# A linear-attention and mixture-of-experts kernel: the diagonal of the scores by two-column products from r*k instead of scaled copies of r

## The chip, the core and the metric

The kernel runs on one core of a Trainium2 chip. A core has five engines with a queue of instructions each: TensorE (PE in the profile; its weight loads are PEld), VectorE (DVE), ScalarE (ACT), GpSimd (POOL) and SyncE (SP), which here issues most of the transfers (DMA). They work at the same time and wait for one another by semaphores. SBUF is the memory on the chip, PSUM the one that TensorE writes. The metric is the device time of one execution in microseconds (us).

## The reference

r, k and v have the shape (4 sequences, 8 heads, 768 tokens, 48). The first half is a recurrence for each sequence and head, with a state of 48x48, a decay w and a bonus u for the token itself:

```python
for t in range(S):
    cur = einsum('bhd,bhe->bhde', u[None] * kt, vt)
    y[:, :, t] = einsum('bhd,bhde->bhe', rt, state + cur)
    state = w[None, :, :, None] * state + einsum('bhd,bhe->bhde', kt, vt)
```

The second half sends the 3072 resulting rows of 384 values through a mixture of experts: a row takes part if its product with w_skip is above 0; it goes to the one of 8 experts with the largest gate value, y = relu(x w1) w2 with 1024 hidden values, and y, weighted by the gate, is added to it.

## The kernel before

**Steps.** The scan cuts the 768 tokens into 12 chunks of 64 and takes two sequences at a time: 2 x 12 = 24 steps, numbered n = 0 to 23. In a step the recurrence becomes products of matrices. The 8 heads are 4 pairs `hp` with two halves `a`; 48 dimensions are padded to 64, so the two halves of a pair fill 128 partitions. `q` is the sequence within the pair of sequences.

**One step.** `prep_r` and `prep_k` multiply the loaded r and k (tile `dm`) by powers of the decay (`w_d`) and make `rd` and `kd`. `scores` multiplies `kd` by `rd` into the PSUM tile `ps_p`, 16 products of 64x64 weights in four quarters of the array. `mask_scores` copies from there into `am` what lies where a token looks at an earlier one (mask `below`) and, for the token itself, from a second half of the columns (mask `eye`). That second half is the product with r times the bonus: `rd` holds two versions of r side by side, and the second is made from the first by VectorE for two head pairs (second part of `prep_r`, L420) and by ScalarE for the other two (`bonus`, L406). `across` adds the products of `rd` with the carried state `sblk` to `ps_y`, `within` those of `am` with v (tile `vz`); `evac` copies `ps_y` out and sends it to memory. `turn_k` transposes `kd` into `ps_l`, and ScalarE copies it to `kt` for the update of the state in `state` (`ps_s`). `turn_x` transposes the finished rows of the step before for the gates. Gates and routing are spread over the steps: gate products every fourth step (L599), parts of the routing on VectorE by the table `DEAL`. From step 4 on pieces of the first expert's weights are loaded too, and ScalarE and one of VectorE and GpSimd split each into two parts (L115, L116).

**Order.** Each engine runs its instructions in the order of the code, which is written out by hand: the block below the definitions is steps 0 and 1, and the loop over n does, in this order, `scores(n + 1)`, `mask_scores(n + 1)`, `across(n + 1)`, the split of a piece, `bonus(n + 2)`, `turn_k(n + 2)`, `turn_x(n)`, `prep_k(n + 3)`, the routing, `prep_r(n + 3)`, `state(n + 1)`, `within(n + 1)` and `evac(n + 1)`. SP issues the loads and stores in the same order. `warm` issues products whose result nobody reads, to keep TensorE going.

**Experts.** After the scan, the rows are gathered by expert, two tiles of up to 128 rows each, and TensorE runs the 8 experts one after the other.

Of the kernel before, what the change touches and what calls it, by code (L numbers as in the profile page):

```python
# [22 lines left out]
P = 128  # L23
# [19 lines left out]
GB = 4  # L43
BH = 2
NDM = 4
# [9 lines left out]
HUGE = 1e30  # L55
FIRST = 4
DEAL = {8: 2, 9: 2, 10: 1, 11: 1, 12: 1, 13: 1, 15: 2, 16: 4, 17: 2, 19: 2, 20: 2}
GROUPS = [(0, 8), (8, 16), (16, 20), (20, 24)]
# [3 lines left out]
def tile_wkv_moe(  # L62
# [183 lines left out]
    with ExitStack() as actx:  # L246
# [7 lines left out]
        def warm(k):  # L254
            for _ in range(k):
                nc.tensor.matmul(ps_t, ones[:, :P], ones, start=True, stop=True)

# [94 lines left out]
        wh_sb = pw[:, NPW - 1, :NHP]  # L352
        uw = tab.tile([DR, NHP], F32, name="uw")
        nc.vector.tensor_tensor(uw, ub_sb, pw[:, 0, :NHP], ALU.mult)

# [43 lines left out]

        rds, kds, kts, kcopy = {}, {}, {}, {}  # L400
        FOUR = ((0, 0), (1, 1), (0, 1), (1, 0))

        def bonus(n, first=0):
            for hp in range(first, NHP):
                rd = rds[n][:, hp]
                nc.scalar.mul(rd[:, :, 1], rd[:, :, 0], uw[:, hp : hp + 1])  # L406

        def prep_r(n, parts=(0, 1)):
            d = loaded[n][0]
            if 0 in parts:  # L410
                rds[n] = wk.tile([DR, NHP, 2, 2, C], F32, tag="rd", name=f"rd{n}", bufs=4)
                nc.vector.tensor_tensor(  # L412
                    rds[n][:, :, :, 0],
                    d[:, 0],
                    w_d[:, n % NSUB, 0][:, :, None].to_broadcast([DR, NHP, 2, C]),
                    ALU.mult,
                )
            if 1 in parts:
                rd = rds[n]
                nc.vector.tensor_tensor(  # L420
                    rd[:, :BH, :, 1],
                    rd[:, :BH, :, 0],
                    uw[:, :BH, None, None].to_broadcast([DR, BH, 2, C]),
                    ALU.mult,
                )

# [10 lines left out]
        def scores(n):  # L437
            kd, rd = kds.pop(n), rds[n]
            for hp in range(NHP):
                for a, q in FOUR:  # L440
                    h = slice(a * C, (a + 1) * C)
                    nc.tensor.matmul(  # L442
                        ps_p[q * C : (q + 1) * C, a, 2 * hp * C : 2 * (hp + 1) * C],
                        kd[h, hp, q, :],
                        rd[h, hp, q].rearrange("p s c -> p (s c)"),
                        start=True,
                        stop=True,
                    )

        def turn_k(n):  # L450
# [7 lines left out]
            kts[n] = kt  # L458

        def mask_scores(n):  # L460
            p = ps_p.rearrange("p a (h s c) -> p (a h) s c", s=2, c=C)
            shape = lambda t: t.rearrange("p a (h c) -> p (a h) c", c=C)
            nc.vector.copy_predicated(shape(am[n % 2]), below, p[:, :, 0])  # L463
            nc.vector.copy_predicated(shape(am[n % 2]), eye, p[:, :, 1])  # L464

# [55 lines left out]
        def across(n):  # L521
            rd = rds.pop(n)
            if n % NSTEP:
                for g in range(NHP // 2):
                    for q in range(NB):
                        for a, c in FOUR:
                            h, hp = slice(a * C, (a + 1) * C), 2 * g + (a ^ c)
                            nc.tensor.matmul(
                                place_y(a, c)[:, q, g, :],
                                rd[h, hp, q, 0, :],  # L530
                                sblk[n % 2][h, q, hp * D : (hp + 1) * D],
                                start=g == q == 0,
                                stop=True,
                                skip_group_check=True,
                            )
# [328 lines left out]
        prep_r(0)  # L864
        bonus(0, BH)
        prep_k(0, nc.vector)
        grow(1)
        square(7)
        square(8)
        turn_k(0)  # L870
        scores(0)
        prep_r(1, (0,))
        prep_k(1)
        bonus(1)
        grow(2, nc.gpsimd)
        mask_scores(0)
        load_dm(4)
        state(0)
        turn_k(1)
        warm(1)  # L880
        within(0)
        evac(0)
        load_v(4)
        nc.sync.dma_start(out=wgp, in_=wgq)
        prep_r(2)
        bonus(2, BH)
        prep_k(2)
        grow(3)
        for n in range(NT - 1):
# [428 lines left out]
```

## Time and profile before

| what | us |
|---|---|
| median of 3 runs | 269.15 (267.34 to 269.96) |
| the profiled execution | 267.03 |
| its span, first to last instruction | 265.2 |
| scores of step 0 to scores of step 1 | 7.40 to 11.66 |
| scores of step 1 to scores of step 23 | 11.66 to 108.50 |
| end of the scan to the first full expert | 113.4 to 131.7 |
| experts | 131.7 to 265.2 |

A row of the timeline gives start, duration, engine, line, operation, output and inputs, shape, and a count if equal instructions are merged; in brackets stands how long the engine had been idle before it, and what ended that. TensorE does a product of 32-bit numbers in two records, so 16 products are `x32`. Records of products overlap, since each includes the time in which the array drains; the pace is read from start to start. A row of the groups by line gives the total and the mean duration (ns), and behind the second bar the idle time before.

### The profile page before, as it was taken

To read this page: it belongs to the slowest core of one execution; us is meant where nothing else is said; L and a number is where in the kernel's file an instruction comes from. 1 tells how busy PE (TensorE), PEld (TensorE's weight loads), DVE (VectorE), ACT (ScalarE), POOL (GpSimd) and SP (SyncE) were. 2 spreads that over 40 slices of the span, in tenths; PEclk is the share of its full clock that TensorE was granted. 3 is DMA by queue.
4 is the path that set the end of the run, shared out by engine and by line. 5 is a ranking of instruction groups with operands and counts; after the bars stand their busy time and mean duration, and the time that the engine had idled before them with its cause. 6 is when DMAs were issued, how large, how long until landed. Compare 5 with 4: busy or idle time off the path is not lost.

```text
span 265.2 us, 8834 instructions
## 1 busy us (share of the span) xinstructions
PE 249.3 (94%) x3594; PEld 229.0 (86%) x3594; DVE 188.9 (71%) x364; ACT 139.7 (53%) x314; POOL 131.9 (50%) x130
## 2 busy tenths in 40 slices
PE   7899999989899999898899999999999999999990
PEld 2799898878798889677698999999999999999990
DVE  8997477897899999674466986998478385692300
ACT  2566658766574766334566707548176282670200
POOL 8666325555655546304785944655535445345011
PEclk9999999999999999999999999999999999999997
DMA  6969798988888887557698796688838566001010
GB/s 213 303 181 259 207 278 248 289 252 244 266 232 264 241 267 205 159 156 262 204 313 261 244 320 230 205 275 253 253 105 279 157 201 222 23 1 46 0 36 24
DMA packets 31142, 54.22 MB, mean 204 GB/s; under 512 B 4536, under 2 KB 14413, under 8 KB 31089
## 3 DMA queue, kind: packets, MB, share of 16 engines
q1 hardware_dynamic: 28896, 48.09, 59.4%
q0 software_dynamic: 2048, 5.44, 6.6%
q8 instruction: 31, 0.51, 0.8%
q14 instruction: 23, 0.18, 0.3%
q10 hardware_dynamic: 144, 0.00, 0.0%
HBM read 45.72 MB, written 8.65 MB: 205 GB/s over the span
## 4 chain that ended last, share of the span: by engine, by line
PE 59%; DVE 8%; DMA 4%; issue 3%; POOL 2%; ACT 1%; SPq 1%; POOLq 0%
PE ps_p L166 11%; PE ps_y L166 11%; PE ps_y L156 5%; PE ps_p L156 5%; PE ps_r L156 5%; PE ps_l L156 5%; PE ps_p L442 3%; PE ps_y L504 2%; DMA dm<-in_dm_dram 2%; DMA raw<-in_w_dram 2%; PE ps_y L218 2%; PE ps_s L475 2%; DVE am L463 1%; DVE ol L768 1%; PE ps_l L455 1%
## 5 line engine op out<-in xcount | busy, mean ns | idle before, releaser
L116 POOL TENSOR_TENSOR lo<-raw,hi 128x512 fp32r<-128x512 f32 x40 | 53.7, 1348 | 43.9 <-ACT hi L115 42.0
L115 ACT CAST hi<-raw 128x512 fp32r<-128x512 f32 x96 | 54.7, 624 | 1.1 <-DMA raw<-in_w_dram 1.1
L116 DVE TENSOR_TENSOR lo<-raw,hi 128x512 fp32r<-128x512 f32 x56 | 50.5, 926 | 2.3 <-ACT hi L115 1.9
L430 POOL TENSOR_TENSOR kd<-dm,w_d 128x512 f32<-128x512 f32 x23 | 33.4, 1455 | 27.2 <-DMA dm<-in_dm_dram 17.8
L174 POOL DMA_INDIRECT out_dram<-xg,sid x16 | 16.8, 1052 | 38.0 <-DVE xg L171 25.7
L124 POOL DMA_INDIRECT xg<-out_dram,gid x16 | 18.1, 1132 | 17.7 <-DMA raw<-in_w_dram 11.9
L442 PE MATMUL ps_p<-rd,kd 64*64 64x128 f32 x768 | 26.7, 276 | 0.1
L463 DVE COPY_PREDICATED am<-below,ps_p 128x512 f32<-128x512 int8 x24 | 17.7, 736 | 11.6 <-PE ps_p L442 11.4
L442 PEld LDWEIGHTS ps_p<-rd,kd 64*64 64x64 f32 x768 | 20.8, 132 | 3.6 <-issue 1.5
L160 ACT ACTIVATE hh<-ps_p 128x464 fp32r<-128x464 f32 x7 | 3.9, 559 | 37.3 <-PE ps_p L156 22.5
L504 PE MATMUL ps_y<-vz,am 128*64 128x96 f32 x384 | 20.4, 248 | 2.3 <-DVE lists L783 0.9
L406 ACT ACTIVATE rd<-rd,uw 128x128 f32<-128x128 f32 x50 | 17.2, 395 | 6.3 <-DVE rd L412 6.1
L457 ACT COPY kt<-ps_l 128x512 f32<-128x512 f32 x22 | 12.9, 586 | 14.3 <-PE ps_l L455 14.1
L504 PEld LDWEIGHTS ps_y<-vz,am 128*64 128x64 f32 x384 | 17.3, 137 | 3.6 <-DVE am L464 1.1
L412 DVE TENSOR_TENSOR rd<-dm,w_d 128x512 f32<-128x512 f32 x24 | 18.8, 782 | 2.2 <-DMA dm<-in_dm_dram 2.2
L475 PE MATMUL ps_s<-vz,kt 128*64 128x96 f32 x352 | 19.6, 252 | 0.0
L166 PE MATMUL ps_p<-hi,hh 128*128 128x384 f32 x56 | 19.4, 347 | 0.0
L166 PE MATMUL ps_p<-hi,hl 128*128 128x384 f32 x56 | 19.0, 339 | 0.0
L166 PE MATMUL ps_y<-hi,hh 128*104 128x384 f32 x56 | 18.9, 338 | 0.0
L166 PE MATMUL ps_y<-lo,hh 128*104 128x384 f32 x56 | 18.9, 337 | 0.0
L166 PE MATMUL ps_y<-hi,hl 128*104 128x384 f32 x56 | 18.9, 337 | 0.0
L166 PE MATMUL ps_p<-lo,hh 128*128 128x384 f32 x56 | 18.8, 336 | 0.0
(239 smaller groups left out, 668.2 us busy)
## 6 DMA issues: line engine op xcount, KB each, us to landing
raw<-in_w_dram SPq DMA_DIRECT2D x96, 256.0 KB
dm<-in_dm_dram SPq DMA_DIRECT2D x24, 512.0 KB
vz<-in_tok_dram SPq DMA_DIRECT2D x48, 96.0 KB
out_dram<-xt SPq DMA_DIRECT2D x48, 96.0 KB
out_dram<-xt SPq DMA_DIRECT2D x4, 192.0 KB
xg<-out_dram,gid POOLq DMA_INDIRECT x16
out_dram<-xg,sid POOLq DMA_INDIRECT x16
wgp<-in_wgq_dram SPq DMA_DIRECT2D x1, 96.0 KB
```

Of the source, the lines that this page charges most:

```text
L115: nc.scalar.copy(hi, t)
L116: eng.tensor_tensor(lo, t, hi.bitcast(F32), ALU.subtract)
L124: ins = nc.gpsimd.indirect_dma_start(out=xg, out_offset=None, in_=out[0:rows], in_offset=bass.IndirectOffsetOnAxis(ap=gid[:, q : q + 1], a ...
L156: nc.tensor.matmul(ph, a[:, c, fs], b[:, c, :], start=(k == 0), stop=(k == 3 * NCC - 1))
L166: nc.tensor.matmul(py, a, b[:, f, :], start=(k == 0), stop=(k == 3 * NFC - 1))
L406: nc.scalar.mul(rd[:, :, 1], rd[:, :, 0], uw[:, hp : hp + 1])
L412: nc.vector.tensor_tensor(rds[n][:, :, :, 0], d[:, 0], w_d[:, n % NSUB, 0][:, :, None].to_broadcast([DR, NHP, 2, C]), ALU.mult,)
L430: (eng or nc.gpsimd).tensor_tensor(kds[n], d[:, 1], w_d[:, n % NSUB, 1][:, :, None].to_broadcast([DR, NHP, 2, C]), ALU.mult,)
L442: nc.tensor.matmul(ps_p[q * C : (q + 1) * C, a, 2 * hp * C : 2 * (hp + 1) * C], kd[h, hp, q, :], rd[h, hp, q].rearrange("p s c -> p (s c)" ...
L463: nc.vector.copy_predicated(shape(am[n % 2]), below, p[:, :, 0])
L475: nc.tensor.matmul(s[a * C : (a + 1) * C, :, hp * D : (hp + 1) * D], kt[:, hp, a, :], t[:, :, a, hp, :], start=i == 0 and hp == 0, stop=Tr ...
L504: ins = nc.tensor.matmul(place_y(a, c)[:, :, g, :], am[n % 2][:, a, hp * C : (hp + 1) * C], t[:, :, a, hp, :], start=g == 0 and n % NSTEP ...
```

## The change

The second half of the score columns goes. `rd` holds one version of r, the score products move 64 columns instead of 128, and the scaled copies on ScalarE and VectorE are gone. In their place `pair` multiplies `rd` by `kd` element by element into `pd`, on VectorE, for steps 0, 13, 17 and 21 on GpSimd. `bonus` is now TensorE's: eight products (4 head pairs, 2 sequences) with `pd` as weights, 128x64, and two columns of `uw` as moving data, one for each half of the partitions with zeros in the other. They sum r*k*u over the dimensions and leave one value for each token and head in `own`, eight columns of `ps_p` that the scores no longer write. `mask_own` places them on the diagonal of `am`, each value repeated along 64 columns and masked by `eye`. `uw` is made on GpSimd instead of VectorE. Two warming products are added at each of two places in the start, and the warming products write `ps_r` instead of `ps_t`.

```diff
+ASIDE = (13, 17, 21)
...
-        uw = tab.tile([DR, NHP], F32, name="uw")
-        nc.vector.tensor_tensor(uw, ub_sb, pw[:, 0, :NHP], ALU.mult)
+        uw = tab.tile([DR, NHP, 2], F32, name="uw")
+        nc.gpsimd.memset(uw, 0.0)
+        for a in range(2):
+            h = slice(a * C, (a + 1) * C)
+            nc.gpsimd.tensor_tensor(uw[h, :, a], ub_sb[h], pw[h, 0, :NHP], ALU.mult)
...
-        def bonus(n, first=0):
-            for hp in range(first, NHP):
-                rd = rds[n][:, hp]
-                nc.scalar.mul(rd[:, :, 1], rd[:, :, 0], uw[:, hp : hp + 1])
+        def pair(n, eng=None):
+            pds[n] = wk.tile([DR, NHP, 2, C], F32, tag="pd", name=f"pd{n}", bufs=3)
+            (eng or nc.vector).tensor_tensor(pds[n], rds[n], kds[n], ALU.mult)
+
+        own = ps_p[:, 0, C : C + 2 * NHP]
+
+        def bonus(n):
+            pd = pds.pop(n)
+            for hp in range(NHP):
+                for q in range(NB):
+                    nc.tensor.matmul(
+                        own[q * C : (q + 1) * C].rearrange("p (a h) -> p a h", a=2)[:, :, hp],
+                        pd[:, hp, q, :],
+                        uw[:, hp, :],
+                        start=True,
+                        stop=True,
+                    )
...
-                        ps_p[q * C : (q + 1) * C, a, 2 * hp * C : 2 * (hp + 1) * C],
+                        ps_p[q * C : (q + 1) * C, a, 2 * hp * C : (2 * hp + 1) * C],
                         kd[h, hp, q, :],
-                        rd[h, hp, q].rearrange("p s c -> p (s c)"),
+                        rd[h, hp, q, :],
...
+        def mask_own(n):
+            t = am[n % 2].rearrange("p a (h c) -> p (a h) c", c=C)
+            nc.vector.copy_predicated(t, eye, own.unsqueeze(2).to_broadcast([P, 2 * NHP, C]))
...
-            nc.vector.copy_predicated(shape(am[n % 2]), eye, p[:, :, 1])
...
             mask_scores(n + 1)
+            if n:
+                mask_own(n + 1)
             across(n + 1)
...
-            if 0 < n and n + 2 < NT:
-                bonus(n + 2, BH)
+            if n + 2 < NT and n + 2 not in ASIDE:
+                pair(n + 2)
...
-                prep_r(n + 3, (0,))
+                prep_r(n + 3)
+                if n + 3 in ASIDE:
+                    pair(n + 3, nc.gpsimd)
             back = state(n + 1)
-            if n + 3 < NT:
-                prep_r(n + 3, (1,))
+            if n == 0:
+                bonus(1)
+                mask_own(1)
...
             within(n + 1, kcopy.get(n + 2, xcopy[n]))
+            if n + 2 < NT:
+                bonus(n + 2)
             evac(n + 1)
```

TensorE in a full step, here from the scores of step 7 up to those of step 8 (a number behind a name is only the tile's buffer). Before:

```order
L442 MATMUL ps_p<-rd_677,kd_675 64x128 x16
L528 MATMUL ps_y<-sblk_198,rd_677 64x48 x16
L455 MATMUL ps_l<-ident,kd_754 128x128 x4
L571 MATMUL ps_t<-ident,xt_776 128x128 x3
L475 MATMUL ps_s<-vz_130,kt_748 64x2x48 x8
L504 MATMUL ps_y<-vz_130,am_150 64x2x48 x8
```

After, with the two-column products of the next step at the end:

```order
L449 MATMUL ps_p<-rd_723,kd_721 64x64 x16
L538 MATMUL ps_y<-sblk_200,rd_723 64x48 x16
L462 MATMUL ps_l<-ident,kd_807 128x128 x4
L581 MATMUL ps_t<-ident,xt_836 128x128 x3
L485 MATMUL ps_s<-vz_130,kt_801 64x2x48 x8
L514 MATMUL ps_y<-vz_130,am_150 64x2x48 x8
L426 MATMUL ps_p<-uw,pd_881 64x2 x8
```

The order of the rest is kept; each step has eight products more, behind within and ahead of the next scores.

VectorE in the start, from r of step 0 to the first mask of step 1. Before:

```order
L412 TENSOR_TENSOR rd_201<-dm_131,w_d 128x8x64
L420 TENSOR_TENSOR rd_201<-rd_201,uw 128x4x64
L430 TENSOR_TENSOR kd_206<-dm_131,w_d 128x512
L325 TENSOR_TENSOR w_d<-w_d,pw 128x512
L338 TENSOR_TENSOR pw<-pw 128x16 x2
L412 TENSOR_TENSOR rd_233<-dm_133,w_d 128x8x64
L463 COPY_PREDICATED am_149<-below,ps_p 128x512
L464 COPY_PREDICATED am_149<-eye,ps_p 128x512
L412 TENSOR_TENSOR rd_277<-dm_137,w_d 128x8x64
L420 TENSOR_TENSOR rd_277<-rd_277,uw 128x4x64
L325 TENSOR_TENSOR w_d<-w_d,pw 128x512
L463 COPY_PREDICATED am_150<-below,ps_p 128x512
```

After, from the first mask of step 0 to the diagonal of step 1:

```order
L474 COPY_PREDICATED am_149<-below,ps_p 128x512
L469 COPY_PREDICATED am_149<-eye,ps_p 128x512
L409 TENSOR_TENSOR rd_246<-dm_133,w_d 128x512
L418 TENSOR_TENSOR pd_286<-rd_246,kd_248 128x512
L409 TENSOR_TENSOR rd_288<-dm_137,w_d 128x512
L325 TENSOR_TENSOR w_d<-w_d,pw 128x512
L474 COPY_PREDICATED am_150<-below,ps_p 128x512
L418 TENSOR_TENSOR pd_328<-rd_288,kd_290 128x512
L409 TENSOR_TENSOR rd_342<-dm_141,w_d 128x512
L469 COPY_PREDICATED am_150<-eye,ps_p 128x512
```

The masks of step 0 now stand ahead of r of step 1, and two r*k and r of step 3 stand ahead of the diagonal of step 1. On GpSimd, the work on `uw` and the r*k of step 0 stand ahead of k of step 1.

More of the change, by code (lines that the diff above doesn't have):

```diff
@@ L43 @@
 GB = 4
-BH = 2
 NDM = 4
@@ L255, in warm @@
             for _ in range(k):
-                nc.tensor.matmul(ps_t, ones[:, :P], ones, start=True, stop=True)
+                nc.tensor.matmul(ps_r, ones[:, :P], ones, start=True, stop=True)
         warm(NWARM)
@@ L398, in setup_routes, with prep_r @@
             )
-        rds, kds, kts, kcopy = {}, {}, {}, {}
+        rds, kds, kts, kcopy, pds = {}, {}, {}, {}, {}
         FOUR = ((0, 0), (1, 1), (0, 1), (1, 0))
-        def bonus(n, first=0):
-            for hp in range(first, NHP):
-                rd = rds[n][:, hp]
-                nc.scalar.mul(rd[:, :, 1], rd[:, :, 0], uw[:, hp : hp + 1])
-        def prep_r(n, parts=(0, 1)):
-            d = loaded[n][0]
[L410 to L425, printed above, removed]
+        def prep_r(n):
+            d = loaded[n][0]
+            rds[n] = wk.tile([DR, NHP, 2, C], F32, tag="rd", name=f"rd{n}", bufs=4)
+            nc.vector.tensor_tensor(
+                rds[n],
+                d[:, 0],
+                w_d[:, n % NSUB, 0][:, :, None].to_broadcast([DR, NHP, 2, C]),
+                ALU.mult,
+            )
[13 more added lines that the diff above has]
+                        stop=True,
+                    )
         def prep_k(n, eng=None):
@@ L458, in turn_k @@
             kts[n] = kt
+        def mask_own(n):
+            t = am[n % 2].rearrange("p a (h c) -> p (a h) c", c=C)
+            nc.vector.copy_predicated(t, eye, own.unsqueeze(2).to_broadcast([P, 2 * NHP, C]))
         def mask_scores(n):
             p = ps_p.rearrange("p a (h s c) -> p (a h) s c", s=2, c=C)
-            shape = lambda t: t.rearrange("p a (h c) -> p (a h) c", c=C)
-            nc.vector.copy_predicated(shape(am[n % 2]), below, p[:, :, 0])
-            nc.vector.copy_predicated(shape(am[n % 2]), eye, p[:, :, 1])
+            t = am[n % 2].rearrange("p a (h c) -> p (a h) c", c=C)
+            nc.vector.copy_predicated(t, below, p[:, :, 0])
         def state(n):
@@ L529, in across @@
                                 place_y(a, c)[:, q, g, :],
-                                rd[h, hp, q, 0, :],
+                                rd[h, hp, q, :],
                                 sblk[n % 2][h, q, hp * D : (hp + 1) * D],
@@ L864, in tile_wkv_moe @@
         prep_r(0)
-        bonus(0, BH)
         prep_k(0, nc.vector)
         grow(1)
+        pair(0, nc.gpsimd)
         square(7)
@@ L871, in tile_wkv_moe @@
         scores(0)
-        prep_r(1, (0,))
+        warm(2)
+        bonus(0)
+        mask_scores(0)
+        mask_own(0)
+        prep_r(1)
         prep_k(1)
-        bonus(1)
         grow(2, nc.gpsimd)
-        mask_scores(0)
         load_dm(4)
         state(0)
+        warm(2)
+        within(0)
+        evac(0)
         turn_k(1)
         warm(1)
-        within(0)
-        evac(0)
         load_v(4)
         nc.sync.dma_start(out=wgp, in_=wgq)
+        pair(1)
         prep_r(2)
-        bonus(2, BH)
         prep_k(2)
```

## The prediction

> **What bounds the kernel now.** I read the page first, then the busy time by stretches, then TensorE's own timeline through one step, then the groups by line and the waits.
>
> ```profile
> PE 249.3 (94%) x3594; PEld 229.0 (86%) x3594; DVE 188.9 (71%) x364; ACT 139.7 (53%) x314; POOL 131.9 (50%) x130
> ...
> PE 59%; DVE 8%; DMA 4%; issue 3%; POOL 2%; ACT 1%; SPq 1%; POOLq 0%
> ```
>
> TensorE is busy for 94% of the span and carries 59% of the chain that ended last. An average hides the stages, so the next view cuts the span: steps 1 to 10 of the scan, steps 11 to 15, steps 16 to the end of the scan, and the experts.
>
> ```profile
> core 0: us, PE busy (x) PEld busy (x) DVE busy (x) ACT busy (x) POOL busy (x), PEclk, DMA share, GB/s
> ...
> 11.66:52.43 40.77, 40.74 (x1080) 36.61 (x1079) 30.76 (x58) 26.99 (x67) 19.34 (x24) 1.00 0.84 244
> 52.43:75.11 22.68, 20.52 (x505) 17.90 (x503) 19.80 (x37) 13.84 (x33) 13.15 (x9) 1.00 0.88 253
> 75.11:113.40 38.29, 36.12 (x907) 31.90 (x905) 34.39 (x77) 23.95 (x59) 19.68 (x15) 1.00 0.78 225
> ...
> 131.70:265.20 133.50, 126.25 (x915) 123.72 (x915) 84.46 (x126) 62.57 (x125) 62.41 (x52) 0.99 0.54 174
> ```
>
> In the first stretch TensorE is busy for 40.74 of 40.77 us, in the next two for 20.52 of 22.68 and 36.12 of 38.29. The granted clock is 1.00 there, so no throttle enters the sum. The change leaves the experts alone; they move as a block when the scan ends earlier or later. One step of the first stretch, on TensorE:
>
> ```profile
> 36.19 1.10 PE L442 MATMUL ps_p<-rd,kd 64*64 64x128 f32 x32
> 37.12 0.63 PE L528 MATMUL ps_y<-sblk,rd 64*64 64x48 f32 x32
> 37.68 0.66 PE L455 MATMUL ps_l<-ident,kd 128*128 128x128 f32 x4
> 38.17 0.49 PE L571 MATMUL ps_t<-ident,xt 128*128 128x128 f32 x3
> 38.59 0.88 PE L475 MATMUL ps_s<-vz,kt 128*64 128x96 f32 x16
> 39.30 0.83 PE L504 MATMUL ps_y<-vz,am 128*64 128x96 f32 x16
> 40.06 1.10 PE L442 MATMUL ps_p<-rd,kd 64*64 64x128 f32 x32
> ```
>
> From start to start (durations overlap by the drain of the last product): scores 0.93, across 0.56, turning of k 0.49, turning of x 0.42, state 0.71, within 0.76, together 3.87 us with no gap. What is added to or taken from TensorE in such a step lengthens or shortens the step.
>
> **The score products.** Each is two records (16 products, 32 records). Halving the moving columns from 128 to 64 doesn't halve 0.93: the across products have the same 64x64 weights, the same count of 32 records and only 48 columns, and take 0.56, or 17.5 ns a record, where in proportion to the columns they would take 0.35. So the weights, not the columns, set their pace, and 64 columns lie between 48 and 128, by this close to 48. I take 0.56: a gain of 0.37 us a step. The ends are 0.56 and 0.93 (no gain).
>
> **The eight products of two columns.** They are 16 records with 128x64 weights, dealt alternately to the two halves of the output rows. The nearest row with such weights and few columns is the gate of one step:
>
> ```profile
> 114.96 0.87 PE L581 MATMUL ps_y<-wgp,xT 128*64 128x18 f32 x12
> 115.77 0.50 PE L196 MATMUL ps_p<-lo,xhl 128*128 128x512 f32 x1
> ```
>
> Twelve records, all in one half, in 0.81 us: 67.5 ns each. Eight records in each half, the halves side by side: 8 x 67.5 ns = 0.54 us. From below the pace of the across products bounds it, 16 x 17.5 ns = 0.28; from above the within products, the same 16 weight loads with 96 columns each, 0.76. I take 0.54, since the kind of row that is nearest in weights and columns gives it. Net: 0.54 - 0.37 = +0.17 us for each step, between -0.09 and +0.39. Steps 2 to 23 (22 of them; 0 and 1 are counted with the start) give +3.7 us, between -2.0 and +8.6.
>
> The Trainium skill (TensorE: Matmul & The Clock Gate, section "LDWEIGHTS (loading the stationary operand)") has the load's time go by the columns of the weights divided by 1.2, whatever the rows. It speaks against this change, since a product of two columns loads as many weights as one of 96. Its estimate here is 53 ns a load and 0.43 us for the eight products, by which the term would be +1.3 us instead. The 67.5 ns of the trace are longer than that, and no run so far shows two columns.
>
> **VectorE, ScalarE and GpSimd in a step.** The groups by line, and two quiet instructions from VectorE's timeline:
>
> ```profile
> 34.89 0.67 DVE L412 TENSOR_TENSOR rd<-dm,w_d 128x512 f32<-128x512 f32 x1
> 35.59 0.42 DVE L420 TENSOR_TENSOR rd<-rd,uw 128x256 f32<-128x256 f32 x1
> ...
> L430 POOL TENSOR_TENSOR kd<-dm,w_d 128x512 f32<-128x512 f32 x23 | 33.4, 1455 | 27.2 <-DMA dm<-in_dm_dram 17.8 <-PE ps_p L442 3.0 <-DVE w_d L325 1.7
> ...
> L412 DVE TENSOR_TENSOR rd<-dm,w_d 128x512 f32<-128x512 f32 x24 | 18.8, 782 | 2.2 <-DMA dm<-in_dm_dram 2.2
> ...
> L420 DVE TENSOR_TENSOR rd<-rd,uw 128x256 f32<-128x256 f32 x23 | 18.1, 787 | 0.7
> L464 DVE COPY_PREDICATED am<-eye,ps_p 128x512 f32<-128x512 int8 x24 | 17.7, 739 | 0.9
> L463 DVE COPY_PREDICATED am<-below,ps_p 128x512 f32<-128x512 int8 x24 | 17.7, 736 | 11.6 <-PE ps_p L442 11.4
> ...
> L406 ACT ACTIVATE rd<-rd,uw 128x128 f32<-128x128 f32 x50 | 17.2, 395 | 6.3 <-DVE rd L412 6.1
> ```
>
> ScalarE loses the 50 copies, 17.2 us. TensorE rarely waits for ScalarE, so this is worth nothing by itself; it enters below, with the waits. VectorE loses the product for two head pairs (787 ns) and gets r*k, of the shape of L412 (782 ns): even. The diagonal's copy keeps its 512 elements and its mask; its source is eight values, each repeated 64 times, instead of 512. I take the old 739 ns, since both masks have the same time. Ends are 0.42 us (the quiet L420, half the elements) and 1.5 us (twice the mask); up to 1.4 it is hidden, because within starts 2.74 us after the scores (the quoted 3.11 less 0.37), and the masks begin when the scores end. Three of the r*k (steps 13, 17, 21) go to GpSimd at 1455 ns each, in steps in which no weight piece is split there; they are needed a whole step later, and that is their cover. Behind each, if it waits for VectorE's r, stands GpSimd's next k. No DMA is added or moved, so SP's queue keeps its order. New is that the two-column products wait for r*k. VectorE makes it right behind the masks, and TensorE is then busy with within for 0.76 us, longer than a quiet r*k; if r*k meets GpSimd and takes 1.4 us, up to 0.6 of it shows, and the scores behind it wait too. I count that inside the range.
>
> **The start.** Steps 0 and 1 are written anew.
>
> ```profile
> 3.34 3.59 POOL L319 MEMSET vz<- 64x384 f32 x8
> ...
> 7.44 1.32 POOL L430 TENSOR_TENSOR kd<-dm,w_d 128x512 f32<-128x512 f32 x1 [0.51 <-POOL vz L319]
> ...
> 8.73 1.49 POOL L325 TENSOR_TENSOR w_d<-w_d,pw 128x512 f32<-128x512 f32 x1
> ...
> 10.06 0.73 DVE L464 COPY_PREDICATED am<-eye,ps_p 128x512 f32<-128x512 int8 x1
> 10.29 1.30 POOL L430 TENSOR_TENSOR kd<-dm,w_d 128x512 f32<-128x512 f32 x1
> ...
> 10.69 1.45 DVE L412 TENSOR_TENSOR rd<-dm,w_d 128x512 f32<-128x512 f32 x1
> 10.85 0.88 PE L504 MATMUL ps_y<-vz,am 128*64 128x96 f32 x16 [0.73 <-DVE am L464]
> ...
> 14.78 0.88 PE L504 MATMUL ps_y<-vz,am 128*64 128x96 f32 x16
> ```
>
> The first r*k is GpSimd's, behind its zeroing (to 6.93) and three small operations on uw, for which I allow 0.4, a little under the 0.51 of the gap ahead of 7.44: 7.35 to 8.65. The products end at 9.2, the mask at 10.0, so within of step 0 comes 0.4 us earlier than 10.85. But r of step 1 then starts at 10.0 on VectorE beside GpSimd's 1.49 us table product, and the row at 10.69 shows what that does: 1.45 us instead of 0.68, ending 0.55 after GpSimd's own. So scores of step 1 start near 12.0. Then across, the turnings and state (0.56 + 0.56 + 0.49 + 0.42 + 0.71) end at 14.8, the two-column products of step 1 at 15.35, and only then can VectorE place their diagonal (0.73): within of step 1 at 16.1 instead of 14.78. Behind that copy on VectorE stand the masks of step 2, which aren't due yet. That is +1.3; I take +1.2, with +0.6 (no meeting with GpSimd) and +2.4 (two more meetings of 0.6) as ends. The four added warming products fill waits.
>
> **Waits that give way.** Where data come late, more work on TensorE is partly free.
>
> ```profile
> 54.28 0.66 PE L455 MATMUL ps_l<-ident,kd 128*128 128x128 f32 x4 [0.29 <-POOL kd L430]
> ...
> 56.02 0.88 PE L504 MATMUL ps_y<-vz,am 128*64 128x96 f32 x16 [0.55 <-ACT xT L572]
> ...
> 72.34 0.45 PE L528 MATMUL ps_y<-sblk,rd 64*64 64x48 f32 x16 [0.93 <-issue]
> ...
> 86.58 0.68 PE L528 MATMUL ps_y<-sblk,rd 64*64 64x48 f32 x32 [0.24 <-ACT xt L539]
> ...
> 104.76 1.38 DVE L420 TENSOR_TENSOR rd<-rd,uw 128x256 f32<-128x256 f32 x1
> ...
> 107.69 0.88 PE L504 MATMUL ps_y<-vz,am 128*64 128x96 f32 x16 [0.95 <-DVE lists L783]
> ```
>
> They sum to 2.96 us. In the last, the masks were late behind L420's 1.38 us; without it and with an r*k of 0.68 earlier, 0.7 goes. The two behind ScalarE (0.79) lose its copies, and about half of the wait. The first hangs on a late input, which a slower TensorE meets later: 0.2. The 0.93 has no releaser in the trace; I allow 0.2. Together -1.5, between 0 and -3.0.
>
> **Sum.** +3.7 + 1.2 - 1.5 = +3.4 us. The profiled execution took 267.03 us (span 265.2 and 1.8 around it), so 270.4 against it; the median of the three runs is 269.15, 2.1 above it, so 272.5 for a median.
>
> **Rivals.**
> Faster: the two-column products run at the pace of the across products, 0.28 us, because hardly anything streams. For it: in that row loads go at 17.5 ns. Against it: L581. It decides below 0.385 us for the eight (22 x (x - 0.37) = 0.3). Price at 0.28: -2.0 + 1.2 - 1.5 = -2.3, or 266.9; with all 3.0 of the waits gone 265.4. Chance 0.24, 0.15 of it more than 1% faster.
> No change: from step 11 on inputs, not TensorE, set the pace (GpSimd waited 17.8 us for dm in the row above, the DMA share is 0.88 in 52 to 75 us), so only steps 2 to 10 pay: 9 x 0.17 + 1.2 - 1.5 = +1.2, or 270.4. Against it: 36.12 of 38.29 us busy at the end. Chance 0.19, 0.02 of it over 1% slower.
> Much slower: the products cost as much as within, 0.76 (22 x 0.39 = 8.6), or the scores gain little, and r*k or the start add 0.6 more than taken, with 3.0 of waits absorbed: 8.6 + 1.8 - 3.0 = +7.4, or 276.6. Chance 0.14.
> My forecast, 272.5 (by itself 271 to 274.5), has 0.43, of which 0.13 stays within 1%.
>
> A measurement of this kernel tells about 1% (2.7 us) from no change. Faster: 0.15. Same: 0.09 + 0.17 + 0.13 = 0.39. Slower: 0.02 + 0.14 + 0.30 = 0.46. The range reaches from inside the faster case, 266.3, to just short of the much slower one, 276.0, and leaves out some 0.1 at each end.
>
> **What would show it.** In a full step on TensorE: scores to across 0.56, the two-column products 0.54, the step 4.04 instead of 3.87. Within of step 1 near 16.1. The scan's last products 3.4 us later, the experts' stretch unchanged. A step at or under 3.87 makes the forecast wrong by the price of the products; a scan that ends no later in spite of 4.04 makes it wrong by the waits.

## The result, and the profile after

| | kernel before | changed kernel |
|---|---|---|
| median, us (6 runs each) | 269.88 (267.34 to 271.59) | 280.35 (276.87 to 283.33) |
| profiled execution, us | 267.03 | 276.87 |
| its span | 265.2 | 275.0 |

The changed kernel is slower: ratio 1.0336, 95% interval 1.0273 to 1.0398. Ratios, here and below, leave out executions more than 1.5% above the fastest of their kernel, which count as a slower state; of the changed kernel the three from 276.87 to 279.44 us are left. The forecast of 272.5 (266.3 to 276.0) had the sign and missed the size. The profiled execution of the changed kernel is the shortest of its six, which matters below.

The page of the changed kernel, rows of parts 1 to 4:

```profile
PE 254.8 (93%) x3980; PEld 235.7 (86%) x3982; DVE 192.7 (70%) x360; ACT 124.7 (45%) x264; POOL 138.3 (50%) x137
...
PEclk9995999999999999999999999999999999999997
...
q8 instruction: 34, 0.56, 0.9%
...
PE 73%; DVE 14%; issue 4%; DMA 3%; POOL 3%; ACT 1%; SPq 0%; POOLq 0%; DVEq 0%
```

ScalarE lost 15 us of work; by itself that was to be worth nothing, and the time shows no gain from it. VectorE's share of the chain rose from 8% to 14%, and in the fourth of the 40 slices TensorE's granted clock is half. Both point to the start. TensorE's timeline there, and one full step behind it:

```profile
15.67 0.58 PE L426 MATMUL ps_p<-uw,pd 128*64 128x2 f32 x16
19.17 1.21 PE L514 MATMUL ps_y<-vz,am 128*64 128x96 f32 x16 [2.92 <-DVE am L469]
...
21.06 1.14 PE L449 MATMUL ps_p<-rd,kd 64*64 64x64 f32 x32
...
24.64 1.55 PE L485 MATMUL ps_s<-vz,kt 128*64 128x96 f32 x16
...
27.35 0.69 PE L449 MATMUL ps_p<-rd,kd 64*64 64x64 f32 x32
27.87 0.63 PE L538 MATMUL ps_y<-sblk,rd 64*64 64x48 f32 x32
28.43 0.66 PE L462 MATMUL ps_l<-ident,kd 128*128 128x128 f32 x4
28.93 0.49 PE L581 MATMUL ps_t<-ident,xt 128*128 128x128 f32 x3
29.34 0.88 PE L485 MATMUL ps_s<-vz,kt 128*64 128x96 f32 x16
30.06 0.83 PE L514 MATMUL ps_y<-vz,am 128*64 128x96 f32 x16
30.72 0.58 PE L426 MATMUL ps_p<-uw,pd 128*64 128x2 f32 x16
31.23 0.69 PE L449 MATMUL ps_p<-rd,kd 64*64 64x64 f32 x32
```

The full step from 27.35 to 31.23 takes 3.88 us; before it took 3.87. The steady part of the change costs nothing. The scores of step 3 (27.35) however come 7.88 us later than before (19.47). Laid out along the scan:

| stretch, from start of scores to start of scores | before | after | difference |
|---|---|---|---|
| start to step 2 | 15.60 | 21.06 | +5.46 |
| step 2 | 3.87 | 6.29 | +2.42 |
| steps 3 to 23 | 89.03 | 90.68 | +1.65 |
| step 23 to the scan's last products | 4.93 | 5.15 | +0.22 |

The differences sum to 9.75 of the 9.84 us between the two profiled executions; the experts take as long as before.

**Where the start is lost.** VectorE's timeline of the changed kernel:

```profile
9.73 0.74 DVE L474 COPY_PREDICATED am<-below,ps_p 128x512 f32<-128x512 int8 x1 [2.22 <-PE ps_p L426]
...
11.98 1.60 DVE L418 TENSOR_TENSOR pd<-rd,kd 128x512 f32<-128x512 f32 x1
...
14.71 0.74 DVE L474 COPY_PREDICATED am<-below,ps_p 128x512 f32<-128x512 int8 x1
15.34 1.39 DVE L418 TENSOR_TENSOR pd<-rd,kd 128x512 f32<-128x512 f32 x1
16.65 1.74 DVE L409 TENSOR_TENSOR rd<-dm,w_d 128x512 f32<-128x512 f32 x1
18.31 0.71 DVE L469 COPY_PREDICATED am<-eye,ps_p 128x512 f32<-128x512 int8 x1
```

The lower mask of step 1 is done at 15.4 and the products of its diagonal end on TensorE at about 16.2. But the diagonal's copy (18.31) is coded late in the loop, behind r*k of step 2 and r of step 3 on VectorE's queue, 3.1 us in all. Both take twice their quiet time of 0.68 us, and GpSimd works beside them, on k from 14.86 to 17.84. TensorE's within waits for that copy, 2.92 us.

**The clock.** The busy times by stretches of the changed kernel (columns: length; busy us and count of PE, PEld, DVE, ACT, POOL; granted clock; DMA share; GB/s):

```profile
19.00:21.00 2.00, 1.83 (x32) 1.86 (x32) 0.02 (x1) 0.48 (x1) 0.81 (x3) 0.64 0.21 80
21.00:24.00 3.00, 3.00 (x72) 2.89 (x71) 1.70 (x3) 0.00 (x0) 1.95 (x5) 0.50 0.54 90
...
27.35:31.23 3.88, 3.88 (x124) 3.65 (x120) 3.08 (x5) 1.45 (x4) 1.15 (x3) 1.00 0.46 115
```

Right behind the pause the clock is 0.64, then 0.50, and step 2 takes 6.29 us with TensorE busy throughout: 2.42 us lost without any wait. The clock's record has 0.50 from 19.57 to 26.39 and 1.00 on both sides. The Trainium skill (TensorE: Matmul & The Clock Gate, section "Part 1: The HAM clock gate") puts the fall to half at an idle window of about 3.4 us. Here 2.92 us were enough.

### The profile page after: what moved, and what is told of

The parts are those of the page before. It is cut to its first block, busy times and chain, and to the rows that moved or that the text cites. A ratio compares the mean times of both kernels' runs of the same rounds, so it can differ in the third digit from the quotient of the medians.

```text
span 275.0 us, 9565 instructions
## 1 busy us (share of the span) xinstructions
PE 254.8 (93%) x3980; PEld 235.7 (86%) x3982; DVE 192.7 (70%) x360; ACT 124.7 (45%) x264; POOL 138.3 (50%) x137
## 4 chain that ended last, share of the span: by engine, by line
PE 73%; DVE 14%; issue 4%; DMA 3%; POOL 3%; ACT 1%; SPq 0%; POOLq 0%; DVEq 0%
PE ps_p L166 11%; PE ps_y L166 11%; PE ps_y L156 5%; PE ps_p L156 5%; PE ps_r L156 5%; PE ps_l L156 5%; PE ps_p L449 4%; PE ps_y L514 4%; PE ps_s L485 3%; PE ps_p L426 3%; PE ps_l L462 3%; DVE am L469 3%; DVE am L474 3%; DVE pd L418 3%; PE ps_y L538 2%
## 5 line engine op out<-in xcount | busy, mean ns | idle before, releaser
L437 POOL TENSOR_TENSOR kd<-dm,w_d 128x512 f32<-128x512 f32 x23 | 35.2, 1531 | 23.0 <-DMA dm<-in_dm_dram 10.3
L418 DVE TENSOR_TENSOR pd<-rd,kd 128x512 f32<-128x512 f32 x20 | 19.7, 986 | 0.1
L485 PEld LDWEIGHTS ps_s<-vz,kt 128*64 128x64 f32 x352 | 15.8, 140 | 3.3 <-issue 2.7
L469 DVE COPY_PREDICATED am<-eye,ps_p 128x512 f32<-128x512 int8 x24 | 17.7, 738 | 0.9
```

Of the source, the lines that this page charges most:

```text
L418: (eng or nc.vector).tensor_tensor(pds[n], rds[n], kds[n], ALU.mult)
L437: (eng or nc.gpsimd).tensor_tensor(kds[n], d[:, 1], w_d[:, n % NSUB, 1][:, :, None].to_broadcast([DR, NHP, 2, C]), ALU.mult,)
L469: nc.vector.copy_predicated(t, eye, own.unsqueeze(2).to_broadcast([P, 2 * NHP, C]))
L485: nc.tensor.matmul(s[a * C : (a + 1) * C, :, hp * D : (hp + 1) * D], kt[:, hp, a, :], t[:, :, a, hp, :], start=i == 0 and hp == 0, stop=Tr ...
```

## The experiments

Theory: the extra time is the start's, by the copy coded late and the half clock behind it; without them the time is near that of before. The first two experiments test the two halves.

**e1: fill the pause.** Thirteen more warming products on TensorE stand in the pause of step 1, so that TensorE doesn't stand still there.

```diff
             if n == 0:
                 bonus(1)
                 mask_own(1)
+                warm(13)
```

> The changed kernel with 13 more warming products (about 0.21 us each) between the two-column products and within of step 1, where TensorE stood still for 2.92 us; nothing else moves. Theory: the pause itself drops the granted clock to about half from 19 to 26 us, and that is what makes step 2 last 6.29 us instead of 3.87. Then within of step 1 still starts near 19.2 (the diagonal is as late as before), but step 2 lasts 3.9, scores of step 3 start near 24.2 instead of 27.35, the span falls by about 3 us to 272, and the runs scatter less than 276.9 to 283.3. Rival: step 2 is slow because its inputs come late; then step 2 stays near 6.3 and the span near 275.

Measured: 280.33 us median (279.55 to 280.74, 4 runs), ratio 1.0409 (1.0316 to 1.0501). The stretches say that the clock part is right:

```profile
20.30:24.18 3.88, 3.88 (x123) 3.64 (x120) 3.01 (x9) 1.93 (x5) 2.30 (x5) 1.00 0.45 87
```

Step 2 takes 3.88 at clock 1.00, and the scores of step 3 start at 24.18, 3.2 us earlier than in the changed kernel. And yet the time is no shorter: steps 3 to 23 now take 97.39 us instead of 90.68. The waits of TensorE in that stretch (waiting instruction, what it waited for, us in total, times, longest):

```profile
PE ps_p L449 <- issue: 3.4, 6, 0.9
PE ps_y L514 <- issue: 1.6, 3, 0.7
...
PE ps_y L538 <- issue: 0.9, 1, 0.9
PE ps_p L426 <- issue: 0.8, 1, 0.8
```

6.7 us in eleven pauses that no semaphore ends (after: 1.5 in two). Their place in the timeline is odd:

```profile
60.06 0.23 PE L426 MATMUL ps_p<-uw,pd 128*64 128x2 f32 x3
61.06 0.57 PE L426 MATMUL ps_p<-uw,pd 128*64 128x2 f32 x13 [0.78 <-issue]
```

The pause falls inside a run of sixteen equal records, whose inputs had all been there when the third of them ran. This is a new cost, and what it is became the main question.

**e2: the copy early.** The products and the copy of step 1's diagonal move to the place that later steps have for the copy.

```diff
             scores(n + 1)
+            if n == 0:
+                bonus(1)
             mask_scores(n + 1)
-            if n:
-                mask_own(n + 1)
+            mask_own(n + 1)
...
-            if n == 0:
-                bonus(1)
-                mask_own(1)
```

> The changed kernel with the diagonal of step 1 placed right behind its first mask, ahead of r*k of step 2 and r of step 3 on VectorE, and the two-column products of step 1 right behind its scores. Theory: the whole loss of the start is VectorE's order there. Within of step 1 starts near 16.3 instead of 19.17, TensorE has no pause over 1 us, the clock stays at 1.00, scores of step 3 start near 21.5 instead of 27.35, and the span is 269 (time 271). Rival: r*k and r only move their time behind the diagonal, so step 2 starts late for want of r or r*k and gives back over half: scores of step 3 near 24.5, span 272.

Measured: 278.55 us median (273.16 to 282.68, 4 runs). The start is repaired: scores of step 3 at 21.36 instead of 27.35, step 2 in 3.87. Again it is given back: 99.91 us from step 3 to 23 in the profiled execution, which is the longest of the four, 4.1 us above their median. It has 7.0 us of such pauses, and behind the worst of them the granted clock falls as well (0.51 from 86.9 to 90.4):

```profile
84.62 0.50 PE L538 MATMUL ps_y<-sblk,rd 64*64 64x48 f32 x20
86.60 0.43 PE L538 MATMUL ps_y<-sblk,rd 64*64 64x48 f32 x12 [1.48 <-issue]
86.97 1.12 PE L462 MATMUL ps_l<-ident,kd 128*128 128x128 f32 x4
```

**e3: the products twice.** From step 3 on e2 computes its eight products two times, into the same place.

```diff
-            for hp in range(NHP):
+            for hp in [*range(NHP)] * times:
...
-                bonus(n + 2)
+                bonus(n + 2, 2 if n else 1)
```

> The second experiment's kernel with the eight two-column products made twice from step 3 on (the same result is written twice). Theory A: the products cost 0.41 us and the switch of the array's tiling from within to scores about 0.10, which was there before the change too; the second eight cost 0.41, and a full step goes from 3.88 to 4.29, the scan by 21 x 0.41 = 8.6 less what waits absorb. Theory B: no price for a switch, the products cost 0.51 as read from start to start; then 4.39 and 10.7 for the scan. Theory C, the prediction's 0.54: 4.42. If TensorE doesn't set the pace of the steps, the scan grows by less than half of any of these.

Measured: 287.41 us (one run); pauses without a releaser 6.8 us, as in e2. The price of eight products by itself:

```profile
72.17 1.08 PE L426 MATMUL ps_p<-uw,pd 128*64 128x2 f32 x32
73.18 0.92 PE L609 MATMUL ps_l<-xT,wgp 128*32 128x128 f32 x24
```

1.01 us for two sets, against 0.51 for one: the second set costs 0.50, so there is no hidden part in the 0.51, as theory B had it.

**e4: the products behind the scores.** The products of a step stand directly behind its scores.

```diff
-            if n == 0:
-                bonus(1)
+            bonus(n + 1)
...
-            if n + 2 < NT:
-                bonus(n + 2)
```

> The second experiment's kernel with the two-column products of each step made right behind its scores, between scores and across, instead of a step earlier behind within. They then have r*k a step sooner than they need it. Theory A (a switch of tiling costs about 0.10): within takes 0.76 again, the products 0.41 + 0.10 between two other tilings, and a full step is 4.0 to 4.1 instead of 3.88, while the waits for r*k (0.17 to 0.55 each, about 1.3 in all) vanish. Theory B (no price for a switch): full steps stay 3.88 and the scan gains the 1.3.

Measured: 272.83 us (one run). A full step takes 4.18 us, more than either theory expected:

```profile
39.73 0.69 PE L449 MATMUL ps_p<-rd,kd 64*64 64x64 f32 x32
40.35 0.63 PE L426 MATMUL ps_p<-uw,pd 128*64 128x2 f32 x16
40.91 0.68 PE L538 MATMUL ps_y<-sblk,rd 64*64 64x48 f32 x32
41.53 0.66 PE L462 MATMUL ps_l<-ident,kd 128*128 128x128 f32 x4
```

Start to start: scores 0.62 instead of 0.52, products 0.56 instead of 0.51, across 0.62 instead of 0.56, and within 0.76 instead of 0.66. In this order the cut of the array (64x64, 128x64) changes twice more in a step, from scores to products and from products to across, and the step is 0.30 us longer: about 0.15 us for each change. The surprise is the stretch from step 3 to 23: 92.50 us, 7.4 less than in e2 although its steps are 0.3 longer, with 0.4 us of pauses. These are single executions, and the one of e2 is its longest.

**The second theory: TensorE waits for its instructions.** The page's third part has a queue q8 of kind instruction, 34 packets with 0.56 MB in the changed kernel and 31 in the kernel before: 16 KB each. In the experts' stretch of the kernel before such packets follow one another after 235 to 259 of TensorE's records. The Trainium skill (Perfetto Trace Analysis, section "The 4-stage abstract model") says that an instruction has 64 bytes; 16 KB would be 256 by that, and the trace agrees (the places of the pauses, below, give it exactly). So TensorE's program comes in pieces, by the transfer engines that also carry the data. The records of q8 in e1, beside its eleven pauses (times of the profile, us):

| packet ends | pause ends | later by |
|---|---|---|
| 26.5 | 28.0 | 1.53 |
| 36.4 | 37.7 | 1.36 |
| 54.6 | 56.0 | 1.38 |
| 59.8 | 61.1 | 1.26 |
| 64.8 | 66.3 | 1.42 |
| 69.9 | 71.5 | 1.53 |
| 74.8 | 76.4 | 1.64 |
| 80.5 | 81.9 | 1.35 |
| 85.7 | 87.0 | 1.30 |
| 91.2 | 92.6 | 1.38 |
| 110.7 | 112.2 | 1.54 |

Every pause ends 1.26 to 1.64 us after the end of a packet. In the kernel before, which has three such pauses (1.6 us), it is 1.25, 1.53 and 1.69. A full step had 206 records (103 products and as many weight loads) in 3.87 us; now it has 238 in 3.88, so 256 records last 4.2 us instead of 4.8. The expectations below write 244 with some further instructions of its queue; the trace shows two of these in a full step. A rival: the pauses go with the eight products themselves, or with VectorE's r*k.

The places of the pauses decide this. Counted along TensorE's queue, the eleven pauses of e1 stand 512, 1024, seven times 256 and 1024 instructions apart, the three of the kernel before 512 and 768. The profiles of the fifteen kernels in this document have 57 pauses without a releaser between the scores of steps 3 and 23. Within each profile they stand whole multiples of 256 apart, whatever products are there, and each ends 1.20 to 1.69 us after a packet. So they belong to the joints between packets, in the kernel before too, and not to the new products or to r*k. A late packet starts late: on average 2.6 us after TensorE has begun the 256 instructions ahead of it, against 1.5 us where no pause follows. It moves no slower (1.18 and 1.15 us).

**e5: lighter transfers.** e2 with the expert weights' pieces that load during the scan cut to 32 of 512 columns.

```diff
+        if pool is wpool:
+            t = raw[e, j] = light[(e * NPC + j) % NST]
+            nc.sync.dma_start(out=t[:, :32], in_=w12[e, :, j * QC : j * QC + 32])
+            return
```

> e2_early_own, but of each of the 16 expert weight pieces that are loaded while the scan runs only 32 of 512 columns are loaded (the other columns are filled once with ones, so the first experts' output is not the reference's). Theory F (TensorE's pauses of kind issue are waits for its instructions, which come by 16 KB packets of queue q8 among the data transfers): with a quarter of the scan's traffic gone from step 4 on, issue before the scan's TensorE groups falls from 7.0 us to 3 at most, and the scores of steps 3 to 23 span 92 to 96 us instead of 99.91. Rival P (the pauses belong to the eight products or to VectorE's r*k, not to the transfers): issue stays at 6 to 7 us and the stretch at 98 to 101.

**e6: longer instructions, as many.** e2 with 14 of 16 score products at 128 columns.

```diff
+                    m = 1 if a == hp == 0 else 2
-                        ps_p[q * C : (q + 1) * C, a, 2 * hp * C : (2 * hp + 1) * C],
+                        ps_p[q * C : (q + 1) * C, a, 2 * hp * C : (2 * hp + m) * C],
                         kd[h, hp, q, :],
-                        rd[h, hp, q, :],
+                        rd[h, hp].rearrange("p q c -> p (q c)") if m == 2 else rd[h, hp, q, :],
```

> e2_early_own with 14 of the 16 score products moving 128 columns again (both sequences' r; the scores of the second sequence are then made of the first one's r, so the output is not the reference's). As many TensorE instructions as in e2_early_own, but longer ones: a full step should take 3.88 + 14/16 x (0.93 - 0.52) = 4.24 us. Theory F (instructions per us set the pauses): issue falls from 7.0 to 2.5 us at most, and steps 3 to 23 span 92 to 96 us, less than the 99.91 of the kernel with the shorter products. Rival P: the pauses stay and 20 x 0.36 = 7 us are added: about 107.

**e7: fewer, wider products.** e2 with four products of 128 columns.

```diff
-                for q in range(NB):
-                    nc.tensor.matmul(
-                        own[q * C : (q + 1) * C].rearrange("p (a h) -> p a h", a=2)[:, :, hp],
-                        pd[:, hp, q, :],
+                nc.tensor.matmul(
+                    own.rearrange("p (a h) -> p a h", a=2)[:, :, hp],
+                    pd[:, hp].rearrange("p q c -> p (q c)"),
```

> e2_early_own with four products of 128 columns of r*k (both sequences at once) in place of eight of 64; the same numbers in the same places, 16 TensorE records fewer a step (some 228 for 244). Theory F: fewer instructions for the same work, so issue falls from 7.0 to 3.5 us or less and steps 3 to 23 span 92 to 96 us. Rival P: issue 6 to 7 us, 98 to 101. The products' own price is open: between 0.25 us (half of the records at 0.03 us each) and 0.55 (a wider weight load of twice the length).

Measured, with the stretch of steps 3 to 23 and the pauses without a releaser in it from the profiled execution:

| kernel | median us | ratio to before | full step | steps 3 to 23 | pauses |
|---|---|---|---|---|---|
| e5 | 274.41 (4 runs) | 1.0274 (1.02 to 1.0349) | 3.87 | 94.38 | 2.4 |
| e6 | 276.93 (4 runs) | 1.0325 (1.0273 to 1.0376) | 4.28 | 96.27 | 0 |
| e7 | 280.25 (4 runs) | 1.0449 (1.0398 to 1.05) | 4.44 | 101.22 | 2.7 |

One execution of each is profiled: of e2, e6 and e7 the longest of four, of e5 the shortest. In the stretches of e2, e3, e5, e7 and e8 the granted clock also fell to 0.50 for 3.4 us, which costs up to 1.7 us (an estimate, half of the 3.4).

e6 tells most. TensorE has 0.4 us more to do in each of 20 steps, 8 us, and the stretch is still shorter than in e2, the median too (276.93 against 278.55). All its waits from step 3 to 23:

```profile
PE ps_y L515 <- DVE am L470: 0.4, 1, 0.4
PE ps_y L515 <- ACT kt L465: 0.4, 1, 0.4
PE ps_p L426 <- DVE pd L418: 0.3, 1, 0.3
PE ps_r L789 <- ACT lg L627: 0.3, 1, 0.3
```

Not one of kind issue, with the same eight products and the same number of instructions as e2. With the places of the pauses, that rules out the rival that binds them to the products (107 us expected, 96.27 measured). e5 fell as expected, but on its shortest execution against the longest of e2, and it has no control yet. e7 missed: the stretch is no shorter, because four products of 128 columns cost twice as much as eight of 64, 0.98 us:

```profile
45.88 1.05 PE L425 MATMUL ps_p<-uw,pd 128*128 128x2 f32 x8
46.86 0.35 PE L448 MATMUL ps_p<-rd,kd 64*64 64x64 f32 x8
```

It also keeps 2.7 us of pauses with only 222 records in 4.44 us, which the pace of instructions alone doesn't explain.

**e8 and e9.** e8 is e4 with another order of the set-up on VectorE. e9 is e2 with that order and with the four products in float32r, where a product is one record instead of two (r*k and w*u are rounded to it): 214 records a step.

```diff
-        bonus(0)
+        prep_r(1)
         mask_scores(0)
+        bonus(0)
         mask_own(0)
-        prep_r(1)
```

```diff
-            pds[n] = wk.tile([DR, NHP, 2, C], F32, tag="pd", name=f"pd{n}", bufs=3)
+            pds[n] = wk.tile([DR, NHP, 2, C], F32R, tag="pd", name=f"pd{n}", bufs=3)
...
+                nc.tensor.matmul(
+                    own[:, 2 * hp : 2 * hp + 2],
+                    pd[:, hp].rearrange("p q c -> p (q c)"),
+                    uw[:, hp, :],
```

> e4_behind_scores with the set-up's work of VectorE in another order: r of step 1 and the lower mask of step 0 before the two-column products of step 0 (which then wait for the mask, and only the diagonal's mask waits for them). If the first step is late because VectorE stands idle from 7.5 to 9.7 us behind those products: within of step 0 starts at about 10.4 us instead of 11.31, the scores of steps 1 to 3 at about 12.0, 16.2 and 20.4 instead of 12.92, 17.15, 21.33, and the time is some 272 us. Rival: r of step 1 runs beside GpSimd's work, takes 1.8 us instead of 0.68 (as it did at 7.51 in the kernel before), and pushes the masks back; then nothing is won. With nothing else changed the stretch from step 3 to 23 should stay within 91 to 95 us.

> e2_early_own with the start of e8_start and the diagonal by four products of 128 columns, in float32r (r*k and w*u rounded to it; one record for a product instead of two): 24 TensorE records fewer a step than with eight products (some 220 for 244). From the 8 records of 0.98 us in e7_four_products the four should take 0.49, as long as the sixteen do now, so the same full step of 3.9 to 4.0 us with a tenth fewer instructions. Theory F (instructions per us set the pauses): issue 3 us at most, steps 3 to 23 span 91 to 95 us, the time 268 to 273 us. Rival P (the pauses go with the products): issue 6 to 7 us, 98 to 101 us, 276 us or more.

Measured: e8 277.26 us (4 runs), ratio 1.0318 (1.0214 to 1.0422). The start was not won (scores of step 1 at 12.88, in e4 12.92): the diagonal's mask still waits for the products of step 0, and these start at 9.45 us instead of 8.94, since GpSimd's r*k comes later. And with the very order of e4 on TensorE the stretch is 96.17 us with 2.7 us of pauses. So e4's single 272.83 was probably a good execution: with the same order on TensorE the pauses differ from one profile to the next. e9: 273.09 us (6 runs), ratio 1.015 (1.0055 to 1.0245); full step 4.00, steps 3 to 23 in 90.39, no pause of kind issue there, and 31 packets on q8 as before the change. The pauses are gone, as the theory asked; the time is just above its 268 to 273. The four records cost 0.54 us:

```profile
39.33 0.60 PE L426 MATMUL ps_p<-uwdt.float32r,pd 128*128 128x2 f32 x4
39.87 0.69 PE L449 MATMUL ps_p<-rd,kd 64*64 64x64 f32 x32
```

**e10 and e11: the same start, eight products against four.** In both, w*u and r*k of step 0 are made by VectorE, and the products of step 0 stand right behind its scores. e10 has the eight float32 products of e2, e11 the four of e9.

```diff
+        pair(0)
         grow(1)
-        pair(0, nc.gpsimd)
...
         scores(0)
-        warm(2)
         bonus(0)
+        warm(2)
```

> e2_early_own (eight float32 products, TensorE's order as there) with w*u and r*k of step 0 made by VectorE in place of GpSimd, and the products of step 0 right behind its scores. If the late start is the wait of the first masks for r*k of step 0 on GpSimd (there at 8.9 us in e2_early_own, and the masks at 9.7): r*k is there at 7.4, the masks begin at about 8.6, and the scores of step 3 start at about 20 us instead of 21.36. Theory F says that this alone brings little: with 244 TensorE instructions in steps of 3.88 us the pauses stay, issue 4 to 7 us, steps 3 to 23 in 96 to 100 us, and the time 275 to 279 us. Rival P2 (the pauses came of the late start, whose loads and steps stood in another phase): issue 2 at most, 91 to 93 us, 269 to 271 us.

> e9_single_pass (four products in float32r, 220 TensorE instructions a step) with the start of e10_start_eight. Theory F: issue 2 us at most, steps 3 to 23 in 90 to 94 us as in e9_single_pass, the start 1 to 1.5 us shorter than there (scores of step 3 at about 20.3 instead of 21.71), so 270.5 to 272.5 us, and 4 to 7 us less than e10_start_eight, though its full step of 4.00 us is longer by 0.12. Rival P2: no shorter than e10_start_eight.

Measured: e10 276.13 us (271.28 to 278.69, 6 runs), ratio 1.0298 (1.0216 to 1.038); e11 271.49 us (270.18 to 273.7, 6 runs), ratio 1.0119 (1.0057 to 1.0182). The start of e10 is near what was expected: r*k starts at 6.50, the first mask at 8.53, the scores of step 3 at 20.39.

```profile
6.50 0.69 DVE L418 TENSOR_TENSOR pd<-rd,kd 128x512 f32<-128x512 f32 x1
...
8.53 0.74 DVE L474 COPY_PREDICATED am<-below,ps_p 128x512 f32<-128x512 int8 x1 [0.44 <-PE ps_p L426]
```

In e11 they start at 21.34, later than the expected 20.3, mainly because its first scores began at 8.05 instead of 7.22. Of two kernels with the same order, the one with the longer steps (4.00 against 3.88) but a tenth fewer records is 4.6 us shorter in the median, and its runs spread over 3.5 us instead of 7.4. The profiled execution of e10 is the shortest of its six, 271.28, and has only 2.1 us of pauses; its median is 4.9 us above it. Its stretch from step 3 to 23 is 91.31 us, where the theory expected 96 to 100: this profile fits the rival P2, and only the median fits the theory. e11's profile, the longest of its six, has the same 91.31 us and no pause.

**e12 and e13: the control for lighter transfers.** The light pieces of e5 in the kernel before, and in e1, whose four executions agreed within 0.4%.

> The kernel before, with the light weight pieces of e5_light_pieces (32 of 512 columns loaded, the rest ones, so that the first experts' output is not the reference's). Theory F: the kernel before has only 1.6 us of pauses without a releaser between its scores of steps 3 and 23, so it gains 0 to 2 us: 267 to 269.5 us, ratio 0.993 to 1.0. Rival I (lighter transfers help through the inputs, whatever the form of the scores): it gains as much as e5_light_pieces seemed to (4 us), ratio 0.985 or less.

> e1_fill (the changed kernel with thirteen more warming products in the pause of step 1, 280.33 us) with the same light pieces. Theory F: the pauses without a releaser, 6.7 us between the scores of steps 3 and 23, fall to 3 at most, that stretch from 97.39 to 92 to 95 us, the time to 275 to 278. Rival I: the same gain as e12_before_light shows. Rival P (pauses bound to the products): issue 6 to 7 us, 279 to 281.

Measured: e12 266.72 us (12 runs) beside 268.04 for before, ratio 0.9982 (0.9947 to 1.0018). e13 277.15 us (6 runs, 272.34 to 280.07), 3.2 less than e1. But the kernel before, measured along with each, was itself 1.6 us shorter beside e13 (268.04 against 269.64), which leaves 1.6, hardly more than the 1.3 of e12. In the one profile of each the pauses fell from 6.7 to 4.3 us, short of the expected 3, and the stretch from 97.39 to 95.60. So the profiles lean to the theory, but the times don't separate it from rival I: that lighter transfers help the changed kernel more than the one before is not shown.

## Why the prediction was wrong

**The products, +0.17 us a step: mis-sized, too dear.** The scores went to 0.52 (forecast 0.56), the products cost 0.51 (forecast 0.54), and within fell from 0.76 to 0.66, which I had not forecast: what follows it now cuts the array in the same way, and e4, where other products follow, has its 0.76 back. The net is 0.01 a step instead of 0.17, or +0.2 us for the 22 steps instead of +3.7.

**The start, +1.2 us: the step that failed.** Within of step 1 was to come at 16.1 and came at 19.17. I had looked at what stands behind the diagonal's copy on VectorE ("Behind that copy on VectorE stand the masks of step 2"), not at what stands ahead of it: r*k of step 2 and r of step 3, 3.1 us beside GpSimd's work. And both masks of step 0 waited for the products, not one, since the two read one PSUM tile; the first began at 9.73, where I had the second end at 10.0. (In e8, where it is coded ahead of the products, it began at 7.77.) The term was +5.46 up to the scores of step 2 (0.76 of it the clock's, by e1), above its upper end of 2.4. e2 and e10, which change only the order in the start (e10 also makes w*u and r*k of step 0 on VectorE), bring the scores of step 3 from 27.35 to 21.36 and 20.39, 1.9 and 0.9 us behind the kernel before, which is inside the term's range.

**The clock: left out.** The sentence "so no throttle enters the sum" held for the steps of the kernel before, not for a pause that the change makes. The 2.92 us halved the clock, and step 2 lost 2.42 us; e1 gives these back (3.88 instead of 6.29).

**The waits, -1.5 us: not seen.** From step 3 to 23 TensorE waits 4.3 us, before 3.8. Of the five waits that were to give way, the four with a releaser are gone, but others have come, for r*k (0.9 us, three times, the longest at the bound of 0.6) and for what the prediction did not name:

```profile
PE ps_p L426 <- issue: 1.5, 2, 1.3
PE ps_p L426 <- DVE pd L418: 0.9, 3, 0.6
PE ps_r L788 <- DVE vl L747: 0.7, 1, 0.7
PE ps_y L538 <- DVE sblk L497: 0.6, 1, 0.6
```

Of the 1.65 us by which the stretch is longer, waits make 0.4 and the steps' own 0.01 us 0.2; the rest, about 1 us, is not traced to rows.

**The rival "much slower"** was nearest in time (276.6) and wrong in its first reason: the products cost 0.51, not 0.76. Its other part, a dearer start, was right in kind, but it added 0.6 to the start's 1.2 where 4.3 came.

**What no term had: the supply of instructions.** The profiled execution of the changed kernel is its shortest and has 1.5 us of pauses without a releaser, as before the change (1.6). Its median lies 3.5 us above it, and the kernels whose start was repaired showed up to 7.0 us of them. In the two profiled executions the start and the clock make 7.88 of the 9.84 us; yet with the start repaired the medians stay at 276 to 279 (e2, e10), so over all executions the pauses weigh as much. I had taken the 0.93 us "without a releaser" in the kernel before for a wait that more work on TensorE would partly absorb, 0.2 of it; it stands at a joint between packets, like the others. Shown is that all these pauses stand at such joints and end shortly after a packet of q8. That fewer or longer instructions make them rarer is borne out by the medians of e11 against e10 (whose products also differ in type and width) and by profiles without pauses (e6, e9, e11), though e7, with fewer, keeps 2.7 us and e4, with as many, has 0.4. That they shrink with less other traffic is not shown (e12, e13). Open are why one packet starts late and the next does not (e4 against e8, e7), and how the median's 3.5 us divide, since only one execution of each kernel was profiled.

No version beat the kernel before. The nearest, e11, is 1.2% slower: its scores of step 3 start 1.9 us later, and its full step is 0.13 us longer.

## What to carry to other kernels

Count an engine's instructions and not only their time: a change that keeps TensorE's time and adds 15% more instructions can lose several us to their supply, and it shows as pauses of kind issue inside runs of equal instructions, at multiples of 256 along the queue. A wide spread between executions is no sure sign of it (7.4 us in e10, but 1.2 in e1, which has 6.7 us of pauses in its profile). Where a change makes one engine wait for a copy on another, read that engine's queue ahead of the copy, in the program's order and at the doubled times that neighbours cause, above all in the first steps. A pause of TensorE of some 3 us can be paid twice, by itself and by the clock behind it, here 2.92 us and some 3 us more.

## What the hardware showed that was not expected

- TensorE's instructions arrive during the run in packets of 16 KB, one for 256 instructions; the pauses for them stand multiples of 256 apart (57 pauses in twelve profiles) and end 1.2 to 1.7 us after a packet.
- A pause of 2.92 us brought the granted clock to 0.50 for 6.8 us. Shorter ones can be followed by 0.50 for 3.4 us: in e2 one of 1.48 us, after two of 1.02 and 1.11 us within 12 us (the turning of k then took 1.12 instead of 0.66), in e8 one of 1.07 us, 10 us after one of 0.95. In e10 one of 1.04 us was not.
- Float32 products with 64 columns of weights, dealt to the two halves of the output rows, take 31 ns a record; with 128 columns over the whole width 122 ns. Half as many wide products took twice as long.
- A change of the array's cut from one group of products to the next costs about 0.15 us (two more in a step of e4, 0.30 us).
